# Order of the first loads and steps of eight weight conversions in an attention and two-layer kernel

## The chip, the cores and the metric

The kernel runs on one core of a Trainium2 chip. The metric is the device time of one execution in microseconds (us). It was 883.6 us before the change, the median of three runs (882.26 to 883.86).

## What is computed

Sliding-window attention over 4 batches, 8 heads, 576 tokens and a head size of 64, then two layers on the 2304 tokens. All is float32.

```python
scores = scale * np.matmul(q, k.transpose(0, 1, 3, 2))
rel = pos[:, None] - pos[None, :]
bias = slopes[:, None, None] * (-np.abs(rel))[None, :, :]
mask = (rel >= 0) & (rel < 128)
scores = np.where(mask, scores + bias[None], -1e9)
attn = softmax(scores)            # with 1e-9 added to the sum
x = np.matmul(attn, v)            # -> 2304 x 512
h = x @ w_in;  x = np.maximum(0.01 * h, h) @ w_out        # layer 1, 512 -> 2048 -> 512
h = x @ w2_in; x = (h / (1 + np.exp(-1.702 * h))) @ w2_out   # layer 2, same sizes
```

The inputs are doubles in memory; the kernel reads their words and makes float32 of them itself.

## The kernel before

The attention runs in 32 steps, one for 128 queries of four heads (or the 192 queries at the ends of a sequence). Eight groups, numbered n, are made of batch and half of the heads: n = 0 and 1 are batch 0. Steps 0 to 2 belong to group 0, 3 to 5 to group 1, 6 and 7 to the ends of both, 8 to 11 to group 2 and so on (line 287). Work is pipelined over the steps: in step s the loop of `attention` (line 901) emits the scores of step s (TensorE, line 384), the output product of step s-3 (line 469) and the transposes of step s-2 (line 434); then the bias, minimum and exponentials of step s (VectorE line 402, ScalarE line 414), normalisation of step s-1 (GpSimd line 428), evacuation of the transposes (ScalarE line 442), and the high and low parts of the output of step s-3, which are the input x of layer 1 (ScalarE line 489, VectorE through line 149).

The order is written out by hand: each engine, and SyncE's queue of loads, works in the order in which the program emits. A list `later` holds work that is due some ticks ahead (`after`, `tick`, lines 59 to 65). A step has four ticks, and a fifth where a group of layer-1 matmuls is emitted at its end. From step 8 on every step ends with one such group: first products (`mm1`, line 509) in steps 8, 9, 14 and 15, output products (`mm2`, line 536) in steps 10 to 13 and 16 to 19. A group needs its chunk's weights; in time it reads them through semaphores.

A weight is loaded raw (`load_w`, line 136, 512 KB) and converted (`conv_w`, line 185). The conversion is emitted after the fourth tick of the steps in `convs`, one in each. Its operations come at these ticks behind that: absolute value at 0 (ScalarE, line 170), clamp, shift, sign, mask, product at 2 to 6 (VectorE, lines 171 to 179), sum at 7 (GpSimd, line 181), high part at 10 (ScalarE, line 196), low part at 12 (GpSimd, line 149). Conversions 0 and 1 are what the first products of chunk 0 need, 2 and 3 its output products; 4 to 7 the same for chunk 1. Three weights are asked for at the start (`load_first`, line 339); each conversion asks for the next one 8 ticks later (line 953).

The loads of a group are `load_k` (keys), `load_q` (queries) and `load_v` (values, eight transfers). For groups 0 and 1 they stand in `load_first`, the queries of blocks 0 and 1 last, as they are needed in steps 6 and 7; group 2's keys and queries are asked for in step 4, its values in step 5, group 3's keys and queries in step 7 (lines 909 to 921). A load's semaphore is used again by the eighth load after it, which waits for it to land.

Of the kernel before, what the change touches and what calls it, by code (L numbers as in the profile page):

```python
# [33 lines left out]
def attention_mlp_kernel(  # L34
        ctx: ExitStack, tc: tile.TileContext, qin, kin, v, w1i, w1o, w2i, w2o, out):
    nc = tc.nc
# [11 lines left out]
    def tmp(shape, dt, tag, bufs):  # L48
        return part[0].tile(shape, dt, tag=tag, name=tag, bufs=bufs)
# [86 lines left out]
    def load_w(n, p):  # L136
        layer, f = divmod(n, NF)
        spare = window[0] and wconv.index((n, p)) % 3 == 2
        raw = (ys[:, 2560 + 4 * S:3584 + 4 * S].bitcast(U32) if spare else
               tmp([128, 1024], U32, "raw", raws[0]))  # L140
        nc.sync.dma_start(out=raw, in_=wsrc[layer][p][f].bitcast(U32))
        wraw[n, p] = raw
# [158 lines left out]
    def new_qk(n):  # L301
        qkv[divmod(n, 2)] = ((late[:, 0], late[:, 1]) if n == 2 else
                             (tmp([128, 2, S], F32, "q", 2), kbuf[:, n % 2]))


    def load_q(e, n, a, lo, hi):
        b, g = divmod(n, 2)
        for h in range(2):
            d = slice(64 * h, 64 * h + 64)
            src = qin[b, 2 * g + a, d].rearrange("p (m h q) -> p m h q", h=2, q=64)  # L310
            e.dma_start(
                out=qkv[b, g][0][d, a, 64 * lo:64 * hi].rearrange("p (m q) -> p m q", q=64),
                in_=src[:, lo:hi, h])

    def load_k(n, lo, hi):
        b, g = divmod(n, 2)
        nc.sync.dma_start(
            out=qkv[b, g][1][:, :, 64 * lo:64 * hi],
            in_=kin[b, 2 * g:2 * g + 2, :, 64 * lo:64 * hi].rearrange("a p s -> p a s"))
# [4 lines left out]
        for a in range(2):  # L324
            load_q(nc.sync, n, a, 0, NKB)

    def load_v(n, engines=(nc.sync,)):
        b, g = divmod(n, 2)
        vv = tmp([128, 2, NKB, 64], F32, "v", 2) if n else vfirst
        values[b, g] = lambda r, a, kb: vv[64 * r:64 * r + 64, a, kb]  # L330

        for a in range(2):
            for h in range(2):
                for r in range(2):
                    src = v[b, 2 * g + a, 64 * r:64 * r + 64, 0:NQB - r, 64 * h:64 * h + 64]
                    k0 = 64 * (h ^ a)
                    engines[h % len(engines)].dma_start(out=vv[k0:k0 + 64, a, r::2], in_=src)

    def load_first(wz):
        for n in range(2):  # L340
            new_qk(n)
        load_k(0, 0, 4)
        load_q(nc.scalar, 0, 0, 2, NKB)
        load_q(nc.sync, 0, 1, 2, NKB)

        nc.scalar.activation(wz[:, 0:1], wz[:, 1:2], AF.Exp)
        load_k(0, 4, NKB)
        load_v(0, (nc.sync, nc.scalar))
        load_w(*wload.pop())
        load_k(1, 0, 4)  # L350
        for a in range(2):
            load_q(nc.sync, 1, a, 2, NKB)
        load_k(1, 4, NKB)
        load_w(*wload.pop())
        load_v(1)
        load_w(*wload.pop())
        for n in range(2):
            for a in range(2):
                load_q(nc.sync, n, a, 0, 2)

    sp, sm, pp, pt, ot = {}, {}, {}, {}, {}

# [392 lines left out]
    wload = wconv[:4 * CB]  # L755
# [128 lines left out]
    def start():  # L884
        wz = tmp([128, 384], F32, "pt", 3)
        nc.gpsimd.memset(wz, 0.0)
        we = tmp([128, 4, 6], F32, "sm", 3).rearrange("p a b -> p (a b)")
        nc.gpsimd.memset(we, 0.0)
        wp = ps("mm")
        for _ in range(5):  # L890
            nc.tensor.matmul(
                out=wp[:, 0:256], lhsT=wz[:, 0:128], rhs=wz[:, 128:384], start=True, stop=True)
        attention_tiles()
        load_first(we)
        emit_consts()
        for n in range(2 * CB):
            alloc_w(n)

    convs = (1, 3, 4, 6, 8, 9, 11, 12)

    def attention():
        nconv, credit = 0, 0.0
        for s in range(NS + 3):
# [14 lines left out]
            if s < NS and nxt < 2 * B and i == 3:  # L918
                load_v(nxt)
# [107 lines left out]
```

## Time and profile before

| | us |
|---|---|
| median of three runs | 883.6 |
| the profiled execution | 883.73 |
| its span | 881.9 |
| TensorE matmuls busy in the span | 860.4 |
| VectorE, ScalarE, GpSimd busy | 588.6, 425.7, 398.0 |

The span is the time between the first and the last instruction that the profile holds; the execution's own time has some 2 us around it. Times in the rows below are us from the start of the span. Busy time of matmuls is modelled, so a busy TensorE may still work below its peak.

### The profile page before, as it was taken

The page shows a single profiled execution, that of the slowest core. Times are in us where ns is not written, and L with a number is a line of the kernel's source. Part 1 is how long each engine was busy: PE and PEld are TensorE (multiplying, and loading weights), DVE is VectorE, ACT ScalarE, POOL GpSimd, SP SyncE. Part 2 cuts the span into 40 slices and gives each one's busy share as a digit, 9 for nine tenths or more (in the row PEclk, how much of TensorE's full clock was granted, in tenths as well). Part 3 has the DMA queues.
Part 4 walks back from the last instruction along what each step waited for, and adds up shares of the span by engine and source line. Part 5 has one row for each costly group of instructions (what it writes and reads, how often), then busy time and mean ns, then how long its engine had stood idle before and what let it go on. Part 6 is the DMA issues. An engine that isn't in the chain of part 4 may idle for free.

```text
span 881.9 us, 15704 instructions
## 1 busy us (share of the span) xinstructions
PE 860.4 (98%) x5728; PEld 758.4 (86%) x5728; DVE 588.6 (67%) x1214; ACT 425.7 (48%) x1025; POOL 398.0 (45%) x444
## 2 busy tenths in 40 slices
PE   7789999999999999999999999999999999999997
PEld 5568888889898988989888999889989989898896
DVE  5888665469888898989886853674575477323334
ACT  5888875453343433443433666245334445433331
POOL 5987554245455655566454343144144332222321
PEclk7999999999999999999999999999999999999999
DMA  9674530142224442425314354235425516856552
GB/s 198 189 184 85 110 82 29 68 143 72 72 75 162 146 155 72 158 71 185 126 44 160 119 157 146 81 132 156 135 69 156 169 59 179 286 179 205 166 179 72
DMA packets 87436, 115.32 MB, mean 131 GB/s; under 512 B 43328, under 2 KB 53568, under 8 KB 86336
## 3 DMA queue, kind: packets, MB, share of 16 engines
q1 hardware_dynamic: 83568, 113.01, 42.0%
q10 hardware_dynamic: 3792, 1.31, 0.6%
q8 instruction: 46, 0.75, 0.4%
q14 instruction: 30, 0.25, 0.1%
HBM read 86.51 MB, written 27.79 MB: 130 GB/s over the span
## 4 chain that ended last, share of the span: by engine, by line
PE 91%; ACT 3%; DVE 3%; DMA 1%; issue 1%; POOL 1%; SPq 0%; DVEq 0%; ACTq 0%; POOLq 0%
PE mm L686 19%; PE mm L536 12%; PE S L619 11%; PE O L536 10%; PE S L509 10%; PE pt L509 10%; PE pt L619 6%; PE O L686 4%; PE O L619 3%; PE mm L509 3%; PE O L469 2%; PE pt L434 2%; PE S L384 2%; ACT st L414 1%; DMA y<-k 1%
## 5 line engine op out<-in xcount | busy, mean ns | idle before, releaser
L149 POOL TENSOR_TENSOR g<-u,g 128x512 fp32r<-128x512 f32 (+1 forms) x86 | 111.9, 1303 | 119.9 <-ACT g L524 100.5
L181 POOL TENSOR_TENSOR ca<-ca,cb 128x512 f32<-128x512 f32 x59 | 81.1, 1374 | 130.0 <-DVE cb L179 78.0
L702 DVE TENSOR_TENSOR y<-y,mm 128x512 f32<-128x512 f32 x102 | 69.8, 684 | 51.0 <-PE mm L686 49.3
L149 POOL TENSOR_TENSOR g<-sn,g 128x384 fp32r<-128x384 f32 x42 | 43.9, 1059 | 122.9 <-ACT g L524 80.2
L686 PE MATMUL mm<-wB,gm 128*128 128x512 f32 (+1 forms) x288 | 86.9, 390 | 0.0
L686 PE MATMUL mm<-wB,g 128*128 128x512 f32 x252 | 82.2, 390 | 0.0
L645 DVE TENSOR_TENSOR sn<-sn,pt 128x384 f32<-128x384 f32 x48 | 26.6, 554 | 76.7 <-ACT sn L640 52.3
L640 ACT ACTIVATE sn<-S 128x384 f32<-128x384 f32 x72 | 35.2, 489 | 78.4 <-PE S L619 78.4
L546 DVE TENSOR_TENSOR y<-y,mm 128x512 f32<-128x512 f32 (+1 forms) x74 | 46.4, 627 | 36.8 <-PE mm L536 36.2
L686 PEld LDWEIGHTS mm<-wB,gm 128*128 128x128 f32 x288 | 53.9, 188 | 10.8
L536 PE MATMUL mm<-g,wA 128*128 128x512 f32 (+1 forms) x264 | 62.5, 371 | 0.4 <-POOL g L149 0.4
L536 PE MATMUL mm<-g,wB 128*128 128x512 f32 (+1 forms) x264 | 62.2, 371 | 0.0
L173 DVE TENSOR_SCALAR ca<-ca 128x512 uint32<-128x512 uint32 x62 | 57.5, 927 | 0.5
L149 POOL TENSOR_TENSOR gm<-sn,gm 128x384 fp32r<-128x384 f32 x30 | 32.0, 1079 | 56.1 <-ACT gm L524 31.2
L175 DVE SCALAR_TENSOR_TENSOR ca<-raw,ca 128x512 uint32<-128x512 uint32 x62 | 56.7, 914 | 0.6
L619 PE MATMUL pt<-x,wA 128*128 128x384 f32 x288 | 56.7, 334 | 0.0
L619 PE MATMUL S<-x,wA 128*128 128x384 f32 x288 | 56.1, 336 | 0.0
L686 PEld LDWEIGHTS mm<-wB,g 128*128 128x128 f32 x252 | 47.0, 188 | 9.1
L631 ACT ACTIVATE sn<-sn 128x384 f32<-128x384 f32 x72 | 37.2, 517 | 34.2 <-DVE sn L645 34.2
L536 PEld LDWEIGHTS mm<-g,wA 128*128 128x128 f32 x264 | 47.8, 188 | 6.7 <-POOL g L149 0.7
L536 PEld LDWEIGHTS mm<-g,wB 128*128 128x128 f32 x264 | 47.8, 188 | 5.8
L171 DVE TENSOR_SCALAR ca<-ca 128x512 f32<-128x512 f32 x62 | 37.7, 608 | 22.6 <-ACT ca L170 22.6
(150 smaller groups left out, 2069.9 us busy)
## 6 DMA issues: line engine op xcount, KB each, us to landing
wA<-w7d SPq DMA_DIRECT2D x80, 256.0 KB, 3.7
w7d<-c SPq DMA_DIRECT2D x8, 1792.0 KB, 6.0
raw<-w2o SPq DMA_DIRECT2D x16, 512.0 KB, 4.5
raw<-w2i SPq DMA_DIRECT2D x16, 512.0 KB, 3.5
wB<-w7d SPq DMA_DIRECT2D x32, 256.0 KB, 2.8
raw<-w1i SPq DMA_DIRECT2D x15, 512.0 KB, 3.4
raw<-w1o SPq DMA_DIRECT2D x15, 512.0 KB, 3.8
wB<-wod SPq DMA_DIRECT2D x26, 256.0 KB, 3.9
```

Of the source, the lines that this page charges most:

```text
L149: e.tensor_tensor(out=out, in0=in0, in1=in1, op=ALU.subtract)
L171: lambda: nc.vector.tensor_scalar(af, af, F32_MIN_EXP, F32_MAX_EXP, op0=ALU.max, op1=ALU.min),
L173: lambda: nc.vector.tensor_scalar(a, a, 0x07FFFFFF, 3, op0=ALU.bitwise_and, op1=ALU.logical_shift_left),
L175: lambda: nc.vector.scalar_tensor_tensor(out=a, in0=hi32, scalar=0xC0000000, in1=a, op0=ALU.bitwise_and, op1=ALU.bitwise_or),
L181: lambda: nc.gpsimd.tensor_tensor(out=af, in0=af, in1=bf, op=ALU.add),
L509: nc.tensor.matmul(out=h, lhsT=w[:, a, k * 128:(k + 1) * 128], rhs=xt[t][:, b2, k], start=(m == 0), stop=(m == len(ops) - 1),)
L536: nc.tensor.matmul(out=y, lhsT=wt[c * CB + f][:, 2 + a, e * 128:(e + 1) * 128], rhs=gt[r, f][:, b2, :], start=(m == 0), stop=(m == len(ops ...
L546: nc.vector.tensor_tensor(out=acc, in0=acc, in1=y, op=ALU.add)
L619: nc.tensor.matmul(out=out, lhsT=w[:, 256 * a + 128 * k:256 * a + 128 * k + 128], rhs=x[:, b2, k], start=(start and m == 0), stop=(stop an ...
L631: nc.scalar.activation(u, h, AF.Gelu_apprx_sigmoid)
L686: nc.tensor.matmul(out=y[:, 128 * q:128 * (q + cut)], lhsT=gt[i, p, f, t][:, b2, e * 128:(e + 1) * 128], rhs=out_slot(i, f, a)[:, 128 * q: ...
L702: nc.vector.tensor_tensor(out=acc, in0=acc, in1=yv, op=ALU.add)
```

## The change

Two things move. In `load_first`, the first keys of group 1 and its queries are issued ahead of the values of group 0; those go to SyncE's queue alone, where half of them were on ScalarE's; the first two weights follow behind the rest of group 1's keys, then the queries of blocks 0 and 1, the values of group 1 and the third weight. And `convs` puts the eight conversions into steps 3, 4, 6, 7, 10, 11, 12 and 13, where they were in 1, 3, 4, 6, 8, 9, 11 and 12; the loads that hang on them move along.

```diff
-    def load_v(n, engines=(nc.sync,)):
+    def load_v(n):
...
-                    engines[h % len(engines)].dma_start(out=vv[k0:k0 + 64, a, r::2], in_=src)
+                    nc.sync.dma_start(out=vv[k0:k0 + 64, a, r::2], in_=src)
...
         load_k(0, 4, NKB)
-        load_v(0, (nc.sync, nc.scalar))
-        load_w(*wload.pop())
         load_k(1, 0, 4)
         for a in range(2):
             load_q(nc.sync, 1, a, 2, NKB)
+        load_v(0)
         load_k(1, 4, NKB)
         load_w(*wload.pop())
-        load_v(1)
         load_w(*wload.pop())
         for n in range(2):
             for a in range(2):
                 load_q(nc.sync, n, a, 0, 2)
+        load_v(1)
+        load_w(*wload.pop())
...
-    convs = (1, 3, 4, 6, 8, 9, 11, 12)
+    convs = (3, 4, 6, 7, 10, 11, 12, 13)
```

## Rows read from the trace of the kernel before

**Rows 1.** The page's chain that ended last, share of the span by engine.
```profile
PE 91%; ACT 3%; DVE 3%; DMA 1%; issue 1%; POOL 1%; SPq 0%; DVEq 0%; ACTq 0%; POOLq 0%
```

**Rows 2.** Stages: stretch, length, PE PEld DVE ACT POOL busy, PE clock, DMA, GB/s.
```profile
35.08:53.19 18.11, 14.47 (x225) 11.44 (x225) 15.54 (x53) 14.98 (x56) 16.90 (x25) 1.00 0.80 202
53.19:81.51 28.32, 25.01 (x404) 21.15 (x404) 22.54 (x101) 24.33 (x93) 23.81 (x36) 1.00 0.57 128
81.51:160.00 78.49, 78.49 (x1209) 65.50 (x1209) 43.37 (x230) 56.89 (x215) 39.87 (x85) 1.00 0.33 78
```

**Rows 3.** TensorE in order of time: start, us, instruction, idle before and its releaser.
```profile
15.37 2.23 PE L384 MATMUL mm<-y,q 64*64 64x192 f32 x14 [1.38 <-DVE sm L402]
...
29.28 1.04 PE L469 MATMUL O<-pt,v 64*64 64x128 f32 x32 [1.42 <-ACT y L414]
...
40.74 2.32 PE L509 MATMUL mm<-x,wA 128*128 128x384 f32 x10 [0.67 <-ACT x L489]
42.99 0.88 PE L384 MATMUL S<-y 64*64 64x192 f32 x16
...
53.19 1.07 PE L384 MATMUL S<-y 64*64 64x64 f32 x24 [1.61 <-DVE sm L402]
...
81.51 0.88 PE L384 MATMUL S<-y,q 64*64 64x192 f32 x16
```

**Rows 4.** SyncE's queue in order of time: start, us, loads issued.
```profile
3.41 6.17 SPq L337 DMA_DIRECT2D y<-v  x4
...
14.58 5.44 SPq L337 DMA_DIRECT2D v<-v  x8
...
27.17 0.51 SPq L141 DMA_DIRECT2D raw<-w1o  x1
...
32.90 6.41 SPq L337 DMA_DIRECT2D v<-v  x8
39.42 0.54 SPq L141 DMA_DIRECT2D raw<-w1i  x1
```

**Rows 5.** Waits of SyncE's queue to 60 us: us in total, times, longest.
```profile
SPq L337 <- DMA q<-q: 2.7, 1, 2.7
```

**Rows 6.** ScalarE in order of time, from step 7's last exponential.
```profile
38.54 0.47 ACT L414 ACTIVATE st<-st,sm 128x192 f32<-128x192 f32 x1
...
39.54 0.46 ACT L414 ACTIVATE y<-y,sm 128x192 f32<-128x192 f32 x1 [0.44 <-DVE sm L402]
...
40.43 0.42 ACT L489 ACTIVATE x<-O 128x128 fp32r<-128x128 f32 x2
...
43.33 0.68 ACT L170 ACTIVATE ca<-raw 128x512 f32<-128x512 f32 x1 [0.85 <-DMA raw<-w1i]
...
44.42 0.52 ACT L524 ACTIVATE g<-u 128x384 fp32r<-128x384 f32 x1
```

**Rows 7.** GpSimd's groups, 44 to 76 us: count, busy us, mean ns, idle before.
```profile
L428 POOL TENSOR_SCALAR st<-st,sm 128x192 f32<-128x192 f32 x16 | 7.7, 500 | 0.0
...
L181 POOL TENSOR_TENSOR ca<-ca,cb 128x512 f32<-128x512 f32 x2 | 2.9, 1454 | 0.0
...
L149 POOL TENSOR_TENSOR g<-u,g 128x384 fp32r<-128x384 f32 x2 | 2.1, 1058 | 1.2 <-ACT g L524 1.2
L149 POOL TENSOR_TENSOR wA<-ca,wA 128x512 fp32r<-128x512 f32 x1 | 1.4, 1444 | 0.0
```

**Rows 8.** VectorE in order of time: clamps of two conversions, first reductions of steps 14, 15.
```profile
60.58 0.98 DVE L171 TENSOR_SCALAR ca<-ca 128x512 f32<-128x512 f32 x1 [2.85 <-ACT ca L170]
...
65.47 0.59 DVE L171 TENSOR_SCALAR ca<-ca 128x512 f32<-128x512 f32 x1
...
71.46 0.34 DVE L402 CUSTOM_DVE_ANT_0 y<-S,bias 128x192 f32<-128x192 f32 x1
...
74.49 0.23 DVE L402 CUSTOM_DVE_ANT_0 st<-S,biasp 128x64 f32<-128x64 f32 x1 [0.59 <-PE S L384]
```

**Rows 9.** Busy time and TensorE's clock in one early stretch, columns as above.
```profile
15.50:22.00 6.50, 6.50 (x74) 5.02 (x78) 3.77 (x16) 4.33 (x17) 3.14 (x5) 0.50 1.17 234
```

## The prediction, made before the changed kernel was run

> **What bounds the kernel now.** I read the chain of waits first: TensorE holds 91% of what ended last [rows 1]. That share is an average, so the second view is the busy time by stage [rows 2]. From 81.5 us on TensorE is busy in all of the 78.49 us shown, and the later chain is matmuls too; whatever delays it before 81.5 us is carried to the end one for one, and whatever is saved before is too. In the two stages ahead it is not the bound: 14.47 of 18.11 us and 25.01 of 28.32 us are busy, with VectorE, ScalarE and GpSimd near 80 to 90%. There a step of the attention waits by turns for each engine. The change touches only that part, so the question is when step 17 begins its scores, now at 81.51 us [rows 3].
>
> The third view is TensorE in order of time [rows 3], by which a step is known by the start of its scores: step 3 at 15.37, step 9 at 42.99, step 11 at 53.19 us. Then SyncE's queue [rows 4, 5], which issues without a pause that matters until 39.42 us, and ScalarE and GpSimd around steps 7 to 10 [rows 6, 7].
>
> **The change part by part.** One part gains, three lose.
>
> *Start.* Step 3's keys and queries are now issued behind the first values and the first weight: the four value loads on SyncE begin at 3.41 us and hold the queue 6.17 us [rows 4]. TensorE stands idle 1.38 us before step 3's scores [rows 3]. With the new order these loads leave SyncE from 3.41 us on, and I expect the 1.38 us gone. It can't be much more: the first values now all follow on SyncE and are needed by step 3's own output, and the second values move behind eight small query loads. By the mean issue of 0.68 us (5.44 us for 8, [rows 4]), 32 issues lie between 3.41 us and the end of the second values, 21.8 us, with 1.5 us for the hold below: the last is issued near 26 us and lands some 3 us later, near step 6's output, which now starts at 29.28 us [rows 3]. So this part gains 1.3 us (0 to 2.1) as far as step 6 or 7. The first weight's conversion leaves steps 1 to 4, which has the same effect and is not counted again.
>
> *The fourth weight comes too late.* A weight load is put 8 ticks after a conversion. The fourth weight's load hangs on conversion 0, now in step 3, which puts it at the fourth tick of step 5, behind the loads of group 2 (step 4) and of its values (step 5). That is word for word the place that the fifth weight has now: issued at 39.42 us, behind value loads that run 6.41 us from 32.90 [rows 4]. It is converted one step earlier than that one was: conversion 3 is in step 7, where conversion 4 was in step 8. And conversion 4 already waits 0.85 us for its weight, until 43.33 us [rows 6].
>
> When does it land? From 3.41 to 39.42 us SyncE makes 43 issues, 29.2 us at 0.68; 6.8 us of the 36.0 are holds, of which 2.7 are one wait for an earlier query load to land [rows 4, 5]. After the change there are 46 issues up to there (four more values, one weight fewer), 31.3 us. If only a 1.5 us hold remains, the load is issued at 36.2 and lands, 3.9 us later like the one of 39.42 to 43.33, at 40.1. If all 6.8 us remain, it lands at 45.4. I take 42.2, nearer to the lower end, since key and weight issues last 0.5 us rather than 0.68 (0.51 and 0.54, [rows 4]) and the first hold shortens.
>
> ScalarE reaches conversion 3 when the exponentials of step 7 are done, which is now just after 38.54 us [rows 6], so at about 37.6 us with the gain of the start. It waits there some 4.6 us. Queued behind it on ScalarE are step 8's exponentials, the copies of step 5's output and the evacuation of step 6's transposes; on VectorE the clamp of conversion 3 and behind it the second half of step 8's reductions; and TensorE waits for the copy of step 5's output in the middle of its first layer-1 group, as it does now for 0.67 us until 40.74 [rows 3]. After the weight has landed come the absolute value (0.6 us), and then what now lies between 39.54 [rows 6] and step 9's scores at 42.99 [rows 3]: 3.45 us. So step 9 starts at 42.2 + 0.6 + 3.45 = 46.25 us, 3.3 us later than now (1.2 to 6.5). The start's gain is inside this term: once the DMA decides, it is lost.
>
> *Step 10's output group waits for GpSimd.* Conversions 2 and 3 move to steps 6 and 7. Counting ticks (four a step, five from step 8 on), GpSimd's queue becomes: gate split of group 1, normalisation of step 8, sum of conversion 3, low part of conversion 2, gate split of group 2, normalisation of step 9, low part of conversion 3. Today the low part of conversion 3 stands ahead of that second normalisation. The fourth of the six matmuls of step 10's output group reads it. By means [rows 7] these are 1.06 + 2.0 + 1.45 + 1.44 + 1.06 + 2.0 + 1.44 = 10.45 us; the first starts about 1.0 us after step 9's scores (two ScalarE passes of the kind of 0.52 us, [rows 6]), and 0.7 us of matmuls follow (three, by ten of the same size in 2.32 us, [rows 3]). So step 11's scores come 12.1 us after step 9's; now it is 10.2. Upper bound of the loss 1.9. Lower bound: VectorE has no conversions 4 and 5 in steps 9 and 10 any more, and the 1.61 us in which TensorE waits for VectorE before step 11 [rows 3] would go: -1.6. The chain on GpSimd is read off the order, so I stay near its end, less 0.7 us for normalisations beside a quiet VectorE: +1.2.
>
> *Conversions packed in steps 10 to 13.* All four of chunk 1 now follow each other. On VectorE a step with a conversion lasts 4.89 us (60.58 to 65.47) or 5.99 us (65.47 to 71.46) [rows 8]. From step 11's scores to step 15's first reduction it now takes 74.49 - 53.19 = 21.3 us with two such steps. Four of them, with a first reduction 0.9 us after the scores and 0.6 us of the first clamp done ahead, last 4 x 5.44 + 0.3 = 22.1 us, from 19.9 (all at 4.89) to 24.3 (all at 5.99). That is +0.8 (-1.4 to +3.0); GpSimd's extra sum and low part in steps 15 and 16, 1.45 us each, lie mostly beside it, and I add 0.2. Term: +1.0. Chunk 1's groups keep their steps (14 to 19): the low part of conversion 7 is ready at the first tick of step 16, just in time.
>
> Sum: 3.3 + 1.2 + 1.0 = 5.5 us. The profiled execution took 883.73 us (span 881.9, and 1.83 around it), 0.13 over the median of 883.6; on the median this gives 889.1.
>
> **A rule against the row.** SyncE's issues of 0.5 to 0.7 us each lie end to end for 36 us [rows 4], so a load more on that queue delays all behind it. The Trainium skill (DMA: Bandwidth & Descriptors, "Issuing engines are not separate DMA queues") says that issuing from several engines saves only the sequencer's time, usually small against the transfer. By that rule the four value loads taken from ScalarE's queue would cost nothing, and the sum would be smaller by their 2.7 us, 886.4; by the row it is as above.
>
> **The rivals.**
> A. As summed: 889.1, own range 886 to 891. For it: 0.85 us of waiting at that place today. Chance 0.48.
> B. TensorE's clock also falls. Now, after idle stretches of up to 1.4 us between short bursts, it works at half clock (0.50, the 1.2 GHz level) from 15.5 to 22 us [rows 9]; before 53.19 us 1.61 us of idle left it at full (1.00) [rows 2, 3]. The wait of 4.6 us is longer than all of these. The ten matmuls left of the first group, 2.3 us [rows 3], would last double: +2.3, 891.4. Chance 0.17. The Trainium skill (TensorE: Matmul & The Clock Gate, "Why this matters for your kernels") has a rule of this kind: idle gaps between bursts of matmuls send the clock back to its lower level.
> C. Next to nothing. The weight lands at 40.1 (+1.2), VectorE's relief cancels the GpSimd queue (0), the packed steps run at their short length (-0.3): 884.5. For it: three engines have slack there. Chance 0.19.
> D. Faster. If the fourth weight lands before ScalarE is there, at 37.6 us, that wait is nil; the start's 1.3 us and VectorE's 1.6 us before step 11 are kept, the packing costs 1.0: -1.9, 881.7. Against it: the place in the queue is that of a load which is late today. Chance 0.16. That the earlier keys bring nothing at all, since the first values gate step 3's output, changes A little, for the weight decides there.
>
> **How the numbers follow.** The likeliest is A, 889.1. Leaving out most of D and the ends of B, the range is 881.7 to 892.5. A measurement tells 0.2% (1.8 us) from no change: D is faster, C mostly the same, A and B slower: 0.15, 0.19 and 0.66.
>
> **What would show it.** Right: step 3's scores start 1 to 2 us earlier with no idle before them; ScalarE idle for 3 to 6 us before the fourth absolute value, ended by a weight's DMA; step 9 near 46 us; in step 10 TensorE waiting for GpSimd in its output group; VectorE without gaps in steps 11 to 14; step 17 near 87 us and the same 800 us behind it. Wrong: the weight there in time, TensorE held in step 10 by VectorE or not at all, or a stage after step 17 that differs.

## The result and the profile after

The changed kernel takes 893.71 us, the median of 4 runs (892.47 to 894.45); the kernel before took 883.55 beside it (4 runs). The ratio is 1.0117, 95% interval 1.0104 to 1.0129: 10.2 us slower, where 5.5 were forecast, and outside the forecast's range. The profiled execution took 894.45 us, its span is 892.5, 10.6 more than before. It is the slowest of the four, with a mean granted clock of 0.984; the fastest, at 892.47 us, had 0.989.

Two measures divide these 10.6 us. The first is when a step begins its scores. Before, step 9 began at 42.99, step 11 at 53.19, step 17 at 81.51 [rows 3], and 800.39 us followed to the end of the span. TensorE after, in order of time (start, us, instruction, idle before and its releaser):

```profile
13.11 1.56 PE L384 MATMUL mm<-y,q 64*64 64x192 f32 x16
...
22.27 1.08 PE L469 MATMUL O<-pt,y 64*64 64x128 f32 x32 [2.32 <-DVE x L149]
...
27.34 0.43 PE L469 MATMUL O<-pt,v 64*64 64x128 f32 x2 [0.61 <-DMA v<-v]
...
29.68 1.54 PE L469 MATMUL O<-pt,v 64*64 64x128 f32 x26 [1.16 <-DMA v<-v]
...
36.19 0.95 PE L384 MATMUL S<-y 64*64 64x192 f32 x16
...
45.23 3.57 PE L509 MATMUL mm<-x,wA 128*128 128x384 f32 x10 [5.39 <-ACT x L489]
48.73 0.97 PE L384 MATMUL S<-y 64*64 64x192 f32 x16
...
58.92 1.10 PE L536 MATMUL mm<-g,wA 128*128 128x384 f32 x3 [2.77 <-POOL wA L149]
59.95 1.56 PE L384 MATMUL S<-y 64*64 64x64 f32 x24
...
89.67 1.13 PE L536 MATMUL mm<-g,wB 128*128 128x384 f32 x3 [1.24 <-POOL wB L149]
90.73 1.56 PE L384 MATMUL S<-y,q 64*64 64x192 f32 x16
```

Step 9 is 5.74 us late (48.73), step 11 6.76 (59.95), step 17 9.22 (90.73), and 801.77 us follow, 1.38 more than before. So the stretches lose 5.74, 1.02, 2.46 and 1.38 us; the fourth number is new. The third hides a gain and a larger loss: by the starts of their scores, steps 11 to 14 took 19.58 us for 20.24, steps 15 and 16 11.20 for 8.08. In these two steps GpSimd has hardly a gap left, VectorE has (before, then after, columns as in [rows 2]); VectorE's first reduction of step 15 follows:

```profile
73.43:81.51 8.08, 7.96 (x135) 7.03 (x134) 5.40 (x32) 8.02 (x33) 6.50 (x12) 1.00 0.79 174
```
```profile
79.53:90.73 11.20, 9.31 (x135) 7.23 (x134) 7.12 (x35) 8.73 (x34) 11.12 (x18) 0.96 0.67 143
```
```profile
81.87 0.21 DVE L402 CUSTOM_DVE_ANT_0 st<-S,biasp 128x64 f32<-128x64 f32 x1
```

Step 3 begins 2.26 us earlier than before, and at step 8 (36.19, before 35.08 [rows 2]) nothing of that is left: the group's output waits for x and twice for the second values.

The second measure is the granted clock. These stretches of the kernel after stand right behind the waits of 5.39, 2.77 and 1.24 us (columns as in [rows 2]):

```profile
45.20:48.80 3.60, 3.57 (x14) 3.13 (x16) 2.41 (x6) 1.78 (x7) 0.00 (x0) 0.50 1.29 223
58.90:62.70 3.80, 3.78 (x59) 3.10 (x59) 1.14 (x10) 1.23 (x6) 0.00 (x0) 0.55 0.44 89
89.70:93.40 3.70, 3.70 (x51) 2.96 (x51) 1.48 (x8) 0.61 (x4) 1.99 (x6) 0.54 0.00 0
```

TensorE works there at its 1.2 GHz level (0.50 to 0.55). The ten matmuls at 45.23 take 3.57 us where they took 2.32 [rows 3], and step 11's scores 1.56 where the same group took 1.07.

The longest wait, on ScalarE, and its cause in the chain of waits (start, us, what):

```profile
19.79 0.66 ACT L170 ACTIVATE ca<-raw 128x512 f32<-128x512 f32 x1 [1.52 <-DMA raw<-w1i]
...
43.49 0.66 ACT L170 ACTIVATE ca<-raw 128x512 f32<-128x512 f32 x1 [4.49 <-POOL y L181]
```
```profile
39.28 4.12 DMA raw<-w1o
```

The trace puts the 4.49 us down to GpSimd, but the fourth weight, asked for at 39.28, lands at 43.40, 0.09 us before ScalarE goes on; in the chain it is the DMA that holds the path.

GpSimd from step 9's gate on:

```profile
49.96 1.00 POOL L149 TENSOR_TENSOR g<-u,g 128x384 fp32r<-128x384 f32 x1 [6.57 <-ACT g L524]
50.96 1.63 POOL L428 TENSOR_SCALAR y<-y,sm 128x192 f32<-128x192 f32 x4
52.55 1.28 POOL L181 TENSOR_TENSOR ca<-ca,y 128x512 f32<-128x512 f32 x1
53.78 1.28 POOL L149 TENSOR_TENSOR wA<-y,wA 128x512 fp32r<-128x512 f32 x1
55.02 1.02 POOL L149 TENSOR_TENSOR g<-u,g 128x384 fp32r<-128x384 f32 x1
56.00 1.64 POOL L428 TENSOR_SCALAR st<-st,sm 128x192 f32<-128x192 f32 x4
57.59 1.28 POOL L149 TENSOR_TENSOR wA<-ca,wA 128x512 fp32r<-128x512 f32 x1
```

This is the order that the forecast wrote down, the low part of conversion 3 last; TensorE's group goes on at 58.92.

### The profile page after: what moved, and what is told of

Read it like the earlier page. It is cut to its first block, busy times and chain, and to the rows that moved or that the text cites. A ratio compares the mean times of both kernels' runs of the same rounds, so it can differ in the third digit from the quotient of the medians.

```text
span 892.5 us, 15704 instructions
## 1 busy us (share of the span) xinstructions
PE 865.2 (97%) x5728; PEld 762.5 (85%) x5728; DVE 585.7 (66%) x1214; ACT 426.3 (48%) x1025; POOL 397.4 (45%) x444
## 3 DMA queue, kind: packets, MB, share of 16 engines
q10 hardware_dynamic: 2576, 1.02, 0.4%
## 4 chain that ended last, share of the span: by engine, by line
PE 90%; POOL 3%; DMA 2%; DVE 2%; SPq 1%; issue 1%; ACT 1%; ACTq 0%; DVEq 0%; POOLq 0%
PE mm L686 18%; PE mm L536 12%; PE S L619 11%; PE O L536 10%; PE S L509 9%; PE pt L509 9%; PE pt L619 5%; PE O L686 4%; PE mm L509 3%; PE O L619 3%; PE pt L434 2%; PE S L384 2%; PE O L469 2%; SPq L337 1%; POOL st L428 1%; DMA raw<-w1i 1%
## 5 line engine op out<-in xcount | busy, mean ns | idle before, releaser
L428 POOL TENSOR_SCALAR st<-st,sm 128x192 f32<-128x192 f32 (+2 forms) x100 | 43.9, 458 | 30.0 <-PE O L469 6.0
```

The source lines that it names most:

```text
L428: nc.gpsimd.tensor_scalar(w, w, sm[s][:, 3, m:m + 1], 1.0, op0=ALU.mult, op1=ALU.mult)
```

## The experiments

Fifteen kernels were run on four chips; each ratio is against runs of the kernel before on the same chip (medians there 883.05, 883.16, 882.90 and 883.03). "Step 9, 11, 17" is when these steps begin their scores, in us of the profiled execution.

| kernel | us | ratio (95%) | step 9 | 11 | 17 |
|---|---|---|---|---|---|
| before | 883.55 | | 42.99 | 53.19 | 81.51 |
| after | 893.71 | 1.0117 (1.0104 to 1.0129) | 48.73 | 59.95 | 90.73 |
| convs_only | 891.87 | 1.0094 (1.0074 to 1.0113) | 46.48 | 58.14 | 89.55 |
| loads_only | 886.83 | 1.0044 (1.0030 to 1.0057) | 47.72 | 57.19 | 85.45 |
| first_four | 894.47 | 1.0129 (1.0114 to 1.0144) | 45.63 | 62.75 | 90.99 |
| last_four | 883.45 | 1.0006 (0.9997 to 1.0015) | 42.63 | 50.41 | 81.04 |
| w4_early | 891.14 | 1.0084 (1.0064 to 1.0104) | 46.79 | 58.02 | 89.06 |
| w4_first | 889.41 | 1.0076 (1.0060 to 1.0092) | 45.78 | 57.22 | 89.29 |
| warm | 894.72 | 1.0124 (1.0108 to 1.0140) | 49.92 | 61.36 | 91.78 |
| warm_full | 892.40 | 1.0104 (1.0087 to 1.0120) | 47.86 | 59.14 | 90.02 |
| lo_first | 889.46 | 1.0068 (1.0053 to 1.0083) | 48.91 | 58.29 | 87.50 |
| w4_first_lo | 884.95 | 1.0029 (1.0018 to 1.0040) | 42.73 | 52.93 | 82.90 |
| spread | 889.33 | 1.0066 (1.0052 to 1.0080) | 43.10 | 58.96 | 87.11 |
| lo_dve | 885.77 | 1.0039 (1.0027 to 1.0051) | 42.27 | 51.16 | 83.29 |
| old_v2_later | 883.08 | 0.9999 (0.9990 to 1.0008) | 43.54 | 53.02 | 81.27 |
| last_four_lo | 883.18 | 1.0004 (0.9995 to 1.0012) | 43.02 | 50.80 | 81.00 |
| last_four_dve | 882.92 | 0.9997 (0.9988 to 1.0005) | 43.30 | 51.08 | 80.60 |

**The halves of the change.** convs_only is the kernel before with the change's `convs`; loads_only is the changed kernel with the old ones; first_four and last_four move half of the conversions in the kernel before. The new lines below are those of convs_only, first_four and last_four, in this order.

```diff
-    convs = (1, 3, 4, 6, 8, 9, 11, 12)
+    convs = (3, 4, 6, 7, 10, 11, 12, 13)
+    convs = (3, 4, 6, 7, 8, 9, 11, 12)
+    convs = (1, 3, 4, 6, 10, 11, 12, 13)
```

> The new conversion steps with the old order of loads. Theory: the loss comes from the places of the conversions. The fourth weight is then asked for behind group 2's values as in the changed kernel and lands near 43 us, ScalarE waits some 4 us for it at the end of step 7, the output group of step 10 waits for GpSimd some 2.5 us, step 16's some 1 us, so 891 to 895 us. Rival (the new order of loads loses, by second values and first weight that come late): no loss without it, 882 to 886 us.

> The loads in the order of the changed kernel, with the conversions in the steps of the kernel before (1, 3, 4, 6, 8, 9, 11, 12). Theory (the change's loads gain at its start only what step 8's keys and queries take back, and conversion 0 in step 1 now holds ScalarE until the first weight lands near 19.8 us): steps 2 and 3 start up to 4 us later than in the changed kernel, step 8 again near 35 to 37, and the time is 883.5 to 886, small against the 10 us of the whole. Rival (the new order of loads carries a loss of its own, by the late first weight and second values): 887 or above.

> The kernel before with its first four conversions alone in the places of the change (3, 4, 6, 7; the others stay in 8, 9, 11, 12). Theory (the late fourth weight with the half clock, and step 10's output group that waits for the fourth weight's low part, hang on conversions 2 and 3): step 9 near 46.5, step 10's group waits 2.5 us, step 11 near 58, and 28.5 us from there to step 17, 888 to 889. Rival (nearly all of the loss comes from the four in steps 10 to 13): below 886.

> The kernel before with its last four conversions alone in the places of the change (10, 11, 12, 13; the first four stay in 1, 3, 4, 6). Theory (packing costs VectorE's gaps in steps 10 to 13, and the last low part comes late for step 16's output group): step 11 as in the kernel before, step 11 to step 17 some 29.8 to 30.8 us instead of 28.3, a wait near 1.2 us for GpSimd in step 16, and half clock behind it that costs up to 1.4 us: 885 to 887. As recorded ahead of the result the packing was put at 1.0 us: 884.1 to 884.5. Together with first_four's loss it should give convs_only's 8.8 us if the parts add.

Moving the conversions alone loses 8.8 us and shows both waits. The chain and TensorE in convs_only:

```profile
36.90 4.25 DMA raw<-w1o
```
```profile
42.98 3.57 PE L509 MATMUL mm<-x,wA 128*128 128x384 f32 x10 [2.56 <-ACT x L489]
46.48 1.56 PE L384 MATMUL S<-y 64*64 64x192 f32 x16
...
57.41 0.79 PE L536 MATMUL mm<-g,wA 128*128 128x384 f32 x3 [2.59 <-POOL wA L149]
```

The new loads on top of it cost 1.8 us more by the medians, though the intervals of the two ratios overlap: with them the weight is asked for 2.38 us later (39.28 for 36.90) and lands 2.25 later (43.40 for 41.15). loads_only lost 3.9 us, more than expected, by waits of which the changed kernel has one, and that only in small. Conversion 0 stays in step 1 and holds ScalarE for the first weight; conversion 2 stays in step 4 and holds it for the third, which now follows the second values. The chain of waits ahead of step 9 runs through both loads:

```profile
18.44 0.66 ACT L170 ACTIVATE ca<-raw 128x512 f32<-128x512 f32 x1 [6.64 <-DMA raw<-w1i]
...
31.32 0.67 ACT L170 ACTIVATE y<-y 128x512 f32<-128x512 f32 x1 [2.05 <-DMA y<-w1o]
```

So neither part is good by itself, and they aren't independent: 8.8 and 3.9 don't add to 10.2.

The other two missed what they were meant to show, and are the more useful for it. last_four, the packing alone, costs nothing measurable. Its step 11 begins 2.78 us earlier than before, for conversions 4 and 5 are gone from steps 8 and 9; behind step 11 it then takes 30.63 us for 28.32. first_four loses 11.6 us, more than all eight together, since conversions 2 to 5 now lie in steps 6 to 9. ScalarE and TensorE in first_four:

```profile
53.20 0.66 ACT L170 ACTIVATE y<-y 128x512 f32<-128x512 f32 x1 [2.84 <-POOL wA L149]
```
```profile
61.49 1.33 PE L536 MATMUL mm<-g,wA 128*128 128x384 f32 x3 [5.82 <-POOL wA L149]
```

Conversions 2 and 5 use one scratch tile (`x % 3 == 2` in `conv_w`), so conversion 5 holds ScalarE until GpSimd is through with the low part of 2. The gate of step 9's first products is queued behind it on ScalarE, and on GpSimd the sum of conversion 4, a normalisation and then the low part of 3 behind that gate. The sum of the halves (12.1) is more than both together (8.8): the places of the last four save 2.8 us of what the first four cost.

**The fourth weight.** Two edits ask for it earlier in the changed kernel, without touching a conversion: in w4_early group 2's values are asked for one step later, in w4_first its keys and queries two steps later as well.

```diff
-            if s == 5:
+            if s == 6:
                 load_v(2)
...
-                if s in (4, 7):
+                if s in (6, 7):
                     load_qk(2 + s // 7)
```

> The changed kernel with group 2's values asked for in step 6, behind the fourth weight, instead of step 5. Theory: the weight is issued near 32.5 us and lands before 38 us, ScalarE's wait of 4.49 us and TensorE's 5.39 us before its ten matmuls go, these take 2.3 us instead of 3.57; step 9 starts near 43 us instead of 48.73, and step 10 and later keep their waits: 888 us (886.5 to 889.5). Rival (the packed conversions set the loss, and time won in step 8 is given back in steps 11 to 16): 892 to 894 us.

> The changed kernel, but both the second group's last keys and queries (step 4's loads) and the third group's values (step 5's) are asked for in step 6, so that the fourth weight follows the third on SyncE's list. Theory (the late fourth weight takes 5.7 us up to step 9, half clock on the ten matmuls in it): SyncE starts the weight near 28.3 us instead of 39.28, it lands near 33 to 35 us, ScalarE does not wait for it, the ten first matmuls of the next projection wait under 2 us and take about 2.3 us, step 9 starts near 43.5 to 45 (the keys and queries themselves land 1.5 to 2 us later, step 8 near 38), and the whole is 888 to 890. Rival (the packing of conversions 2 and 3 in steps 6 and 7 costs this whichever way the weight comes, through ScalarE's and GpSimd's own work): step 9 stays near 46 to 48 and the time at 891 or above.

w4_early missed its 888 us: the weight was asked for 5.59 us earlier and landed only 1.78 earlier (chain of waits):

```profile
33.69 7.93 DMA raw<-w1o
```

It lay behind group 2's keys and queries, issued just ahead of it from 29.71 us on (in w4_first one of these queries took 7.09 us to land), so the time fell by 2.6 us and not by 5.7. That these loads held it, and not the values issued behind it, no run separates. In w4_first it follows the third weight (issued 28.25) and ScalarE doesn't wait for it any more. 4.3 us are saved by the medians. The profiled execution is the longest of its four (892.21): TensorE waited 1.23 us for group 2's queries in it, the twelve matmuls of its first group took 3.60 us, and step 9 began at 45.78; in w4_first_lo, which is the same up to there, at 42.73. That is the kernel before's 42.99: without the late weight nothing of the 5.74 us is left.

**The clock.** Before the first group of first products, matmuls of no use were put into the changed kernel, 22 in warm and 33 in warm_full; the group's first real matmul overwrites what they leave.

```diff
+        for _ in range(WARM if r == (0, 0, 0) and ff == 0 else 0):
+            nc.tensor.matmul(
+                out=h, lhsT=w[:, 0, 0:128], rhs=xt[t][:, 0, 0], start=True, stop=True)
```

> The changed kernel with 22 matmuls more, whose result is overwritten, ahead of the first layer-1 group, in the 5.39 us that TensorE waits in step 8. Theory (the idle stretch lowers TensorE's clock): the ten matmuls behind take 2.3 us instead of 3.57 and step 9 starts 1.2 us earlier: 892.4 us (892 to 893). Rival (the clock is low for another reason): 893.7 us or, as the matmuls cost time, above.

> The changed kernel with 33 matmuls of no use ahead of the first projection group of the next pair (22 in warm), enough to fill TensorE's whole wait for the fourth weight. Theory (it is TensorE's idleness ahead of them that halves the clock of the ten matmuls): they run at full clock in about 2.3 us instead of 3.57, step 9 starts 1.2 us earlier than in the changed kernel, and the time is about 892.5. Rival (the half clock hides under the wait for other work, so that the clock costs nothing here): no change, 893.7 or above.

22 were too few: TensorE stood idle for 1.97 us behind them, and the ten matmuls ran at half clock as ever. With 33 the idle time is 0.56 us (TensorE and the stretch in warm_full, where lines 489 and 509 have moved to 490 and 513):

```profile
39.04 5.98 PE L509 MATMUL mm<-x,wA 128*128 128x384 f32 x33
44.85 0.51 PE L513 MATMUL mm<-x,wA 128*128 128x384 f32 x2
45.92 2.01 PE L513 MATMUL mm<-x,wA 128*128 128x384 f32 x10 [0.56 <-ACT x L490]
```
```profile
45.90:47.90 2.00, 1.98 (x14) 1.73 (x14) 1.93 (x6) 1.76 (x7) 0.00 (x0) 1.00 1.25 259
```

Full clock (1.00), 2.01 us for 3.57, step 9 0.87 us earlier, and a median 1.3 us lower, as expected, though the intervals of the two ratios overlap. So it is the idle time ahead of them that halves the clock of the ten. At this one place it costs 0.87 us at step 9, of which 0.71 are left at step 17.

**Step 10's output group.** lo_first puts the low parts of conversions 3 and 7 one tick earlier, ahead of the normalisation that they stood behind; w4_first_lo joins it to w4_first; lo_dve then gives these two to VectorE (the second pair of lines).

```diff
-            (12 if early else 8, lambda: (
+            ((11 if x in (3, 7) else 12) if early else 8, lambda: (
...
-                sub(nc.gpsimd if early else nc.vector, lo, af, hi.bitcast(F32)),
+                sub(nc.gpsimd if early and x not in (3, 7) else nc.vector, lo, af, hi.bitcast(F32)),
```

> The changed kernel with the low parts of conversions 3 and 7 one tick earlier, so that on GpSimd they stand ahead of the normalisation of step 9 and of the gate split ahead of step 16's group. Theory: TensorE's wait of 2.77 us in step 10 falls to 1.1, that of 1.24 us in step 16 to near 0.3, and with shorter idle stretches the half clock behind them goes: 2.5 to 4 us off, 890 to 891.5 us. Rival (normalisation is late instead, and TensorE waits for the transposes): no change, 893 to 894.5 us.

> The kernel of w4_first with lo_first's edit (the low parts of conversions 3 and 7 one tick earlier). Theory (the weight and step 10's output group are two separate terms that add): 4 us less than w4_first, 884 to 886. Rival (the first makes room that the second needs too, so that they share their gain): less than 2 us below w4_first, 886.5 or above.

> The kernel of w4_first_lo, with the low parts of conversions 3 and 7 subtracted by VectorE instead of GpSimd. Theory (the 1.8 us left are the 1.57 us that TensorE waits in step 10 for GpSimd): the wait in step 10 is gone or under 0.5 us, step 11 starts 8.5 to 9.2 us after step 9 instead of 10.20, step 17 near 81.5 to 82, and the time is 883.0 to 884.0. Rival (VectorE is the bound there as well, and pays with the subtraction what GpSimd saves): no change, 884.9.

lo_first saves 4.25 us with an edit that changes no amount of work. TensorE and the stretch behind its wait in lo_first:

```profile
57.56 0.79 PE L536 MATMUL mm<-g,wA 128*128 128x384 f32 x3 [1.15 <-POOL wA L149]
58.29 0.89 PE L384 MATMUL S<-y 64*64 64x64 f32 x24
```
```profile
57.56:62.00 4.44, 4.44 (x79) 3.84 (x83) 3.20 (x17) 3.84 (x17) 2.92 (x7) 1.00 0.43 96
```

The wait falls from 2.77 to 1.15 us and the clock stays at full; step 16's wait of 1.24 becomes 0.17 and 0.34, and the stage behind step 17 takes 800.40 us again. Both edits together save 8.8 us, where singly they saved 4.3 and 4.25: the two causes add, and 1.8 us over the kernel before are left.

lo_dve shows where those are not. Step 11 begins 8.89 us after step 9 instead of 10.20, as expected of step 10's wait, but by step 17 the gain is gone (83.29 for 82.90), and the time is no lower. VectorE and GpSimd at the second packed conversion, first in w4_first_lo, then in lo_dve:

```profile
59.09 0.43 DVE L171 TENSOR_SCALAR y<-y 128x512 f32<-128x512 f32 x1
```
```profile
59.13 1.52 POOL L181 TENSOR_TENSOR ca<-ca,cb 128x512 f32<-128x512 f32 x1 [1.09 <-DVE cb L179]
```
```profile
58.50 1.51 DVE L171 TENSOR_SCALAR y<-y 128x512 f32<-128x512 f32 x1
```
```profile
58.44 1.29 POOL L181 TENSOR_TENSOR ca<-ca,cb 128x512 f32<-128x512 f32 x1 [1.09 <-DVE cb L179]
```

The clamp takes 0.43 us where it starts first and 1.51 where GpSimd does, by hundredths of a us; the last section has the other traces. In lo_dve the next clamp, at 64.37, takes 1.41 as well, 0.14 us behind a start of GpSimd; together 2.06 us more on the engine that the scores of steps 13 and 14 wait for (1.55 and 0.41 us).

**The packing.** spread is w4_first_lo with the last four conversions back in their old steps.

```diff
-    convs = (3, 4, 6, 7, 10, 11, 12, 13)
+    convs = (3, 4, 6, 7, 8, 9, 11, 12)
```

> The kernel of w4_first_lo, with conversions 4 and 5 back in steps 8 and 9, and 6 and 7 in 11 and 12, where the kernel before has them. Theory (what is left of the loss, 1.8 us, is four conversions one step behind the other in steps 10 to 13, which leave VectorE no gap there): step 11 to step 17 takes 28.3 to 28.6 us instead of 29.97, and the time is 883.0 to 883.8, the same as the kernel before. Rival 1 (it is the conversions of steps 3 to 7, whose work is pushed on behind step 11): no change, 884.9. Rival 2 (the loads in the new order give time back once nothing waits for a weight): below 882.5.

It loses 4.4 us more, but not where the theory looked. From step 11 to step 17 it takes 28.15 us for 29.97, a little under what was expected, so the packing does cost 1.8 us there. All of it lies in steps 15 and 16 (7.99 us for 10.41). In w4_first_lo GpSimd has no gap there, VectorE has, and GpSimd holds 83% of the chain of waits from 60 to 84 us. The stretch in w4_first_lo:

```profile
68.00:82.00 14.00, 12.65 (x199) 10.32 (x195) 11.54 (x50) 11.25 (x42) 14.00 (x18) 1.00 0.61 129
```

What spread loses lies ahead of step 11: 15.86 us from step 9 for 10.20. ScalarE waits 2.83 us for the fifth weight at 44.82, and as in first_four, conversion 5 in step 9 holds ScalarE for the scratch tile (2.96 us), the gate comes late, and the low part of conversion 3 stands behind the gate on GpSimd. Step 10's group waits three times, the last time for that low part:

```profile
57.70 1.33 PE L536 MATMUL mm<-g,wA 128*128 128x384 f32 x3 [2.40 <-POOL wA L149]
```

**Better than both?** old_v2_later is the kernel before with `load_v(2)` in step 6, last_four_lo is last_four with lo_first's edit, last_four_dve that with the subtraction on VectorE.

> The kernel before with the third group's values asked for in step 6 instead of step 5, so that the fifth weight goes ahead of them. Theory (in the kernel before, ScalarE waits 0.85 us for that weight at 43.33 us, and the weight's place on SyncE's list is what sets this): the wait is gone, and 0.3 to 0.9 us of it reach the end: 882.6 to 883.2. Rival (ScalarE has slack there, since step 9 waits for other work): no change, 883.5.

> The kernel of last_four with the low parts of conversions 3 and 7 one tick earlier. Theory (packing the last four gives 2.4 us before step 11 and takes 2.3 behind it, of which 1.2 is step 16's wait for GpSimd): that wait is under 0.6 us, step 17 near 80.3 instead of 81.04, and the time is 882.2 to 882.9, up to 0.8 below last_four and at or below the kernel before. Rival (step 17 waits for VectorE then): no change against last_four, 883.4.

> The kernel of last_four_lo, with those two low parts on VectorE as in lo_dve. Theory: as lo_dve, nothing left to wait for GpSimd in steps 10 and 16; step 17 near 80, 881.8 to 882.6, the fastest so far. Rival (VectorE, without gaps in steps 11 to 14, passes its own time on): as last_four or slower, 883.4 or above.

All three are the same as the kernel before within their intervals. In old_v2_later ScalarE's 0.85 us of waiting [rows 6] is gone, and TensorE waits 0.66 us for x all the same: it was covered. last_four_dve begins step 17 0.9 us earlier than before and shows only 0.1 in the median. No version faster than the kernel before was found.

## Why the prediction was right or wrong

The direction, the two waits and their order in time were right; the size was half. Two steps of sum A failed. It put TensorE's lower clock behind the waits at nothing, where half clock cost 1.25 us ahead of step 9 and as much in step 17. And in the packing it put GpSimd's extra sum and low parts in steps 15 and 16 at 0.2 us, where 1.84 were lost behind VectorE's part. Step 10's term and VectorE's part were near, the weight's landing 1.2 us off.

**Start (forecast 1.3 us, lost later).** Step 3 gained 2.26 us and step 5 4.51 (19.07 for 23.58), more than forecast, and the loss came earlier too: the first weight held ScalarE 1.52 us at 19.79, the second values held step 6's output (0.61 and 1.16). That it is worth nothing by step 9 was right.

**The fourth weight (forecast +3.3, measured +5.74).** The cause is right: w4_first with lo_first's edit begins step 9 where the kernel before does. The term was mis-sized twice. The weight landed at 43.40, not 42.2, inside the bounds given (40.1 to 45.4), for the value between them was taken near the lower one: 1.2 us, of which 1.0 is the issue. And the 3.45 us from there to step 9 were taken from rows at full clock; they took 4.58, since the ten matmuls alone were 1.25 us longer at half clock. That was rival B, put at a chance of 0.17 beside A. It should have stood in A's sum: a forecast wait of 4.6 us was itself the condition of B, and the evidence, half clock between short bursts [rows 9], was in the text. B's own price, 2.3 us for the ten, was too high: they took 3.57 us, not double the 2.32.

**Step 10 (forecast +1.2, measured +1.02).** The mechanism is the chain written down. GpSimd took 8.91 us from the gate split to the end of conversion 3's low part (49.96 to 58.87), where 9.75 were forecast (10.45 less 0.7); it began 1.23 us after step 9's scores instead of 1.0, and the three matmuls behind it took 1.10 us at half clock instead of 0.7. That these misses nearly cancel is luck. The bound for VectorE's relief was too small: last_four takes 7.78 us from step 9 to step 11 for 10.20, 2.4 us gained where at most 1.6 were allowed. Of the 3.4 us between that and the 11.22 of the changed kernel, lo_first's one tick takes back 1.84 (9.38).

**Packing (forecast +1.0, measured +2.46 up to step 17).** VectorE's part was right: step 15's first reduction came 21.92 us after step 11's scores (81.87 less 59.95) where 22.1 were forecast and 21.3 had been; last_four has 22.10. What failed is the 0.2 us for GpSimd behind it. From that reduction to step 17's scores it took 8.86 us for 7.02, 1.84 more: the sum and the low parts don't "lie mostly beside it" where GpSimd is busy for 11.12 of 11.20 us, and step 16's group waits 1.24 us for conversion 7's low part, which was to be "just in time". last_four shows the same by itself, 8.53 us for 7.02 and a loss of 2.31 from step 11 to step 17. And the same packing gives the relief of the term before, so that alone it costs nothing; the text named both effects and never set them against each other as one move.

**Behind step 17 (forecast 0, measured +1.38).** "Whatever delays it before 81.5 us is carried to the end one for one" left out that the clock is carried too: up to 93.4 us the stage ran at 0.54, and step 17 alone took 4.59 us for 3.34. lo_first, with 0.51 us of waiting in step 16 instead of 1.24, has 800.40 us there. But so have convs_only and last_four, within 0.2 us, with waits of 1.24 and 1.23 us and full clock behind them, so this part isn't settled by the wait's length.

So half clock, at three places and in no term of A, is about half of the missing 5 us: 1.25 at the first, 1.25 of the 1.38 behind step 17, and a share not separated from the wait at step 11.

**The rule against the row.** The row came nearer. In the changed kernel, which differs from convs_only in its loads alone, the weight is asked for 2.38 us later, near the 2.7 us of the four value loads put onto SyncE (the waits in the queue differ too). Step 9 begins 2.25 us later, of which 1.18 are left at step 17. The Trainium skill (DMA: Bandwidth & Descriptors, "Issuing engines are not separate DMA queues") says that issuing from several engines saves only the sequencer's time, usually small against the transfer. Here it wasn't small: a delay of 2.38 us stands beside the 4.12 us from the weight's issue to its landing.

**Open.** w4_first_lo begins steps 9 and 11 0.26 us earlier than the kernel before and step 17 1.39 us later, so what it keeps of the loss lies in the packed steps. lo_dve shows that taking away step 10's wait doesn't pay, and spread that the stretch comes back when the conversions are spread. That GpSimd's queue in steps 15 and 16 is the cause is read from its busy time and the chain of waits; no run lightened GpSimd there without loading another engine. Why the clock fell behind step 16's wait in one kernel and not in others stays open.

## What to carry to other kernels

When a forecast makes TensorE wait for some microseconds between short bursts, price what follows the wait at the lower clock, in the likeliest case and not in a rival, and look past the stage where you stop summing. Price a stage for every engine that gets more work in it: GpSimd's extra work, put at 0.2 us beside VectorE's, cost 1.84. Work that is moved to a later step leaves a gap where it was: put gain and loss into one term, for the two may cancel as in last_four, and a half of the move may cost more than the whole as in first_four. An earlier issue isn't as much of an earlier landing: in w4_early 5.6 us at the issue brought 1.8 at the landing.

## What the runs showed of the hardware

Half clock followed shorter waits than rival B's 4.6 us. Behind 1.97 (warm), 2.56 (convs_only) and 2.77 us of idle time the granted clock fell to the 1.2 GHz level, and behind 1.57 us in step 10 of w4_first_lo step 11's scores took 1.56 us; before the change, 1.61 us ahead of step 11 left the clock at full [rows 2, 3], and so did 1.15 in lo_first and 0.56 in warm_full. But 1.24 us in step 16, behind other waits in that step, was followed by 0.54 in the changed kernel, and in last_four a wait of 1.23 at the same place was not (its step 17 scores took 0.88 us): the length of the last wait alone doesn't tell.

One VectorE instruction, the clamp of 128 x 512 elements, took 0.43 us or 1.51 us by whether it began 0.04 us before a GpSimd addition or 0.06 us after; in the first case GpSimd's took 1.52 us instead of 1.29. The Trainium skill (SBUF — State Buffer, "Who interferes with whom") states such a lock: with some VectorE instructions, tensor_scalar among them, the engine that issues first holds the shared ports for its whole instruction, and the other stands still. The trace agrees: the clamp that began second ended 0.28 us behind GpSimd's addition (60.01 and 59.73), as if it had stood still up to there. In the 17 traces up to 100 us all 30 clamps of this size that began under a GpSimd addition or subtraction with more than 0.15 us left ended 0.27 to 0.29 us behind it. Of 19 that began up to 0.15 us ahead of one, 18 took 0.41 to 0.43 us; the other, 0.01 us ahead, took 1.57.
